# Other places in the order for loads, maxima, bulk transfers and the norm's chunks in a windowed attention stage

## The chip, the core and the metric

The kernel runs on one core of a Trainium2 chip. Its engines work side by side, each through its own list of instructions in order: TensorE (PE; weight loads are shown as PEld), VectorE (DVE), ScalarE (ACT), GpSimd (POOL) and SyncE (SP). In this kernel every DMA is issued by SP, one after the other. The metric is the time of one execution in microseconds (us) on the device; lower is better. An order of instructions is fixed when the program is built, so what the change moves are places in these five lists.

## The reference, cut to what matters

The input is 2048 rows of 448 numbers. A condition vector gives six modulation vectors. The block normalises the rows, scales and shifts them, applies attention with 16 heads of 28 numbers in which a row sees itself and the 255 rows before it, projects, adds; then it normalises again and applies a dense layer, Mish, a second dense layer, and adds.

```python
idx = jnp.arange(S)                                    # S = 2048, W = 256
mask = (idx[:, None] - idx[None, :] >= 0) & (idx[:, None] - idx[None, :] < W)
scores = jnp.where(mask[None, None], jnp.einsum("bhqd,bhkd->bhqk", q, k) * (Dh ** -0.5), -1e9)
o = jnp.einsum("bhqk,bhkd->bhqd", _softmax(scores), v)  # H = 16, Dh = 28
x = x + ga * (o_as_rows @ wo)
h = _layernorm(x) * (1 + cb) + sb
x = x + gb * (mish(h @ w1 + b1) @ w2)
```

## The kernel before

**Stages.** The rows are worked in four groups `g` of 512. Ahead of the attention loop the weights for queries, keys and values are loaded and the first group's projections are begun. The attention loop then runs over 64 *slots* (group and head: slot i is group i // 16, head i % 16). After it the dense layers run.

**Numbers in two parts.** Products of numbers with 32 bits are made of parts, a high and a low one. Queries and keys are stored to DRAM (`scr`) in three such parts (`qk_out`, L314, whose `put` issues the stores) and read back by slot with `L(i)` (L562): one DMA for q (84 rows), one for k, into 8 buffers each.

**One slot.** `A(i, t)` (L571), t from 0 to 3, multiplies a tile of 128 queries with its 384 keys, and VectorE reduces the product to the maximum of each row. When two slots are through, `M2(pr)` (L584) turns the pair's maxima with TensorE, VectorE writes them in a high and a low part (tile `mr`), and two DMAs put these as rows 84 and 85 into the q buffers of that pair, so that the next product subtracts the maximum by itself. `B(u)` (L601) makes that product, masked, with q and k the other way round, and ScalarE takes the exponential. `PV(w)` (L627) multiplies with the values; `EV`, `E` and `E2` bring the result back and divide.

**The loop.** Four slots are a round q of 12 steps (u = 12 q + r). Step r runs `B` of slot 4q + r % 4, one of its three blocks. So the pair of maxima for slots 4q + 4 and 4q + 5 has its first reader at step 12, and the pair for 4q + 6 and 4q + 7 at step 14. The 16 calls of `A` for the next four slots are spread over steps 1 to 10: those of the first slot at steps 1 and 2, of the second at 3 to 5, of the third at 6 and 7, of the fourth at 8 to 10. `M2` of the first pair stands at step 8, of the second at step 11. Slots 4q + 8 to 4q + 11 are loaded at steps 8, 9, 10 and 11, by `load_slot`, which first makes sure with `need` that their projections are stored. The first eight slots and the first two pairs are handled ahead of the loop.

**Filling work.** Between these, `fill_main(g)` yields chunks of the next group's work (`gen_hT`: transposes of the normalised rows, four chunks; `gen_qkv`: projections; `gen_oT` and `gen_wo`: output projection of the last group), and each chunk names its cost. Each step adds `RATE[g]` (twice that in the first `FRONT[g]` steps of a group) to a credit, and chunks are emitted while it is above zero. `chunk["v"]` is how many products a chunk of `tile_mms` holds; steps 0 and 18 of a group set it. Whatever is left at the end of a group is emitted at once by `drain`. A second list, `fill_early` and `fill_late`, is moved on by one entry a step (`side_step`): loads of x (`x_load`), the norm's statistics (`gen_ln1`), modulation vectors, later the first pieces of `w1`.

**Bulk transfers.** Stores of projections, loads of x rows and weights are not issued where they arise but put on the list `later`; at steps 1 to 8 and 11 of a round one entry is taken from it. `flush` issues all of it. On SP, an instruction that waits for its data holds up all that stand behind it.

Of the kernel before, what the change touches and what calls it, by code (L numbers as in the profile page):

```python
# [51 lines left out]
def adaln_block(ctx: ExitStack, tc: tile.TileContext, x, wqkv, wo, w1, b1, w2, c, w_mod, out):  # L52
# [32 lines left out]
    def bank(tag, bufs, name):  # L85
        return PS[0].tile([128, 512], F32, name=name, tag=tag, bufs=bufs)
# [4 lines left out]
    def x_load(g):  # L91
        xin[g] = qk.tile([128, 4, 512], F32, name=f"xin{g}", tag="xin")
        for t in (0, 2):
            r = g * GT + t * 128
            dma(xin[g][:, t:t + 2, 0:D], xf[r:r + 256, :].rearrange("(t p) d -> p t d", p=128))
# [134 lines left out]
    def tr_chunk(xs, ci, p):  # L230
        for t in range(4):
            PE.transpose(p[:, t * 128:(t + 1) * 128], xs[t][:, ci * 128:(ci + 1) * 128], ident)


    def hT_hi(p, ci, hh, si):
        ACT.activation(hh[:, ci], p, AF.Identity, scale=cols[:, si + 1, ci:ci + 1], bias=cols[:, si, ci:ci + 1])

    def hT_y(p, ci, y, si):
        ACT.activation(y, p, AF.Identity, scale=cols[:, si + 1, ci:ci + 1], bias=cols[:, si, ci:ci + 1])
# [5 lines left out]
    def new_T(key, pl):  # L245
        return (pl.tile([128, 4, GT], F32R, name=f"hh{key}", tag="hh"),
                pl.tile([128, 4, GT], F32R, name=f"hl{key}", tag="hl"))
# [5 lines left out]
    def gen_ln1(g, act=False):  # L253
        def xn_tiles():
            return [xin[g][:, t] for t in range(4)]
        for r in gen_ln([xin[g][:, t, 0:D] for t in range(4)], qk, xn_tiles, f"a{g}", act):
            if r:
                XS[g] = r
            yield "dve"
# [8 lines left out]
    def gen_hT(g):  # L268
        drain(ln1[g])
        hh, hl = HT[g] = new_T(g, mid)  # L270
        for ci in range(4):
            p = bank("mm", 2, f"tr{g}{ci}")
            tr_chunk(XS[g], ci, p)
            y = qk.tile([128, 512], F32, name=f"y{g}{ci}", tag="y", bufs=2)

            def ev(p=p, ci=ci, y=y):
                hT_y(p, ci, y, 0)
                hT_hi(p, ci, hh, 0)

            def lo(ci=ci, y=y):  # L280
                POOL.tensor_tensor(hl[:, ci], y, hh[:, ci].bitcast(F32), op=ALU.subtract)
            pipe.add(2, ev, lo)
            yield 2
        ht_done.add(g)

    def finish():
# [3 lines left out]
    def drain(*gs):  # L290
        for g in gs:
            for _ in g:
                pipe.step()
# [14 lines left out]
    later = []  # L308

    def flush():  # L310
        while later:
            later.pop(0)()
# [176 lines left out]
    def gen_mod_ln2(i):  # L489
        acc = yield from gen_wm_sum(i, qk)  # L490
        yield "bank"
        p = bank("mm", 2, f"mc{i}")
        mod_cols(acc, p)
        mod_cols_out(p, i - 1)
        yield
# [62 lines left out]
    NS = NG * H  # L558
# [3 lines left out]
    def L(i):  # L562
        g, h = divmod(i, H)
        q, k = Q3[i % NQ], K3[i % NK]
        f0, f1 = h * DH, D + h * DH
        q0, k0 = g * GT, max(g * GT - W, 0)
        l0 = k0 - (g * GT - W)
        dma(q[0:84, :].bitcast(F32), scr[f0:f0 + DH, :, q0:q0 + GT].rearrange("d a n -> (d a) n"))
        dma(k[0:84, l0:].bitcast(F32), scr[f1:f1 + DH, :, k0:q0 + GT].rearrange("d a n -> (d a) n"))

    def A(i, t):  # L571
        g, h = divmod(i, H)
        q, k = Q3[i % NQ], K3[i % NK]
        if i % 2 == 0 and t == 0:
            mx[i // 2] = att.tile([128, 2, 4], F32, name=f"mx{i}", tag="mx", bufs=2)
        c0 = max(256 - 128 * t, 0) if g == 0 else 0
        p = bank("sA", 2, f"sA{i}_{t}")
        PE.matmul(p[:, c0:384], q[0:84, t * 128:(t + 1) * 128], k[0:84, t * 128 + c0:t * 128 + 384],  # L578
                  start=True, stop=True)
        DVE.tensor_tensor_reduce(out=junk[:, c0:384], in0=p[:, c0:384], in1=mask[:, c0:384], scale=1.0,  # L580
                                 scalar=-3.0e38, op0=ALU.add, op1=ALU.max,
                                 accum_out=mx[i // 2][:, i % 2, t:t + 1])
# [44 lines left out]
    def PV(w):  # L627
        q, b = divmod(w, 3)
        g, h = divmod(4 * q, H)
        if b == 0:  # L630
            pvb[q] = bank("pv", 1, f"pv{q}")
        for n, (jj, t0, t1, c) in enumerate(by_width(units(g, b))):
            j = 4 * g - 2 + jj
            for a in range(4):
                PE.matmul(pvb[q][32 * a:32 * a + 32, t0 * 128:t1 * 128], V[j % NV][:, h + a, :],  # L635
                          Pt[4 * w + a][:, c:c + 128 * (t1 - t0)],
                          start=(b == 0 and n == 0), stop=False, skip_group_check=True)

    def EV(q):
        O4[q] = att.tile([128, GT], F32, name=f"o4_{q}", tag="o4")  # L640
        ACT.activation(O4[q], pvb[q], AF.Copy)
# [207 lines left out]
    def fill_early():  # L849
        yield from ln1[1]  # L850
        for g, mods in ((2, (gen_mod_wo,)), (3, (lambda: gen_mod_ln2(3), lambda: gen_mod_ln2(4)))):
            while g - 1 not in ht_done:
                yield
            for _ in range(0):
                yield
            later.append(lambda: x_load(g))
            for _ in range(6):
                yield
            flush()
            yield from ln1[g]  # L860
            for m in mods:
                yield from m()
# [8 lines left out]
    def side_step(g, two):  # L871
        i = g == NG - 1
        if not (told.get(i) == "bank" and pipe.held() or told.get(i) == "dve" and two):
            told[i] = next(side[i], None)

    RATE = (0.68, 0.93, 0.93, 0.45)
    FRONT = (0, 2, 2, 0)
    ln1 = {g: gen_ln1(g) for g in range(1, NG)}
    fillers = {g: fill_main(g) for g in range(NG)}
    side = (fill_early(), fill_late())  # L880

    def step(g):
        return next(fillers[g], 99.0) or RATE[g]

    def need(keys, g):
        if all((g, m) in done for m in keys):
            return
        flush()
        while not all((g, m) in done for m in keys):
            pipe.step()  # L890
            try:
                next(fillers[max(g - 1, 0)])
            except StopIteration:
                next(fillers[g])
            flush()

    def load_slot(i):
        if i >= NS:
            return
        g, h = divmod(i, H)  # L900
        f0, f1 = h * DH, D + h * DH
        need({f0 // 128, (f0 + 27) // 128, f1 // 128, (f1 + 27) // 128}, g)
        L(i)
# [21 lines left out]
    for u in range(NU + 7):  # L925
        s, k = divmod(u, 3)
        g = s // H
        if k == 0 and s % H == 0 and 0 < g < NG:
            drain(fillers[g - 1], *side[:g == NG - 1])
            flush()  # L930
        pipe.step()
        w, m = divmod(u - 5, 4)
        if m == 0 and 0 <= w < NU // 4:
            PV(w)
            if w % 3 == 2:
                EV(w // 3)
        if u < NU:
            B(u)
        q, r = divmod(u, 12)
        tiles = [divmod(n, 4) for n in range(16) if 1 + n * 10 // 16 == r and 4 * q + 4 < NS]  # L940
        for a, t in tiles[:1]:
            A(4 * q + 4 + a, t)
        if r in (8, 11) and 4 * q + 4 < NS:
            M2(2 * q + 2 + (r == 11))
        a = (r - 8) % 12
        if a < 4:
            load_slot(4 * ((u - 8) // 12) + 8 + a)
        if r - 3 in (0, 1) and 0 <= (u - 12 - 3) // 12 < NS // 4:
            (E, E2)[r - 3](q - 1)
        if g < NG:  # L950
            v = u - 48 * g
            if v in (0, 18):
                chunk["v"] = 4 if v == 0 and g or 0 < g < NG - 1 else 2
            if v == 0:
                credit = 0.0
            credit += RATE[g] * (2 if v < FRONT[g] else 1)
            while credit > 0.0:
                credit -= step(g)
            if v > 1:
                side_step(g, len(tiles) > 1)  # L960
            if later and r in (1, 2, 3, 4, 5, 6, 7, 8, 11):
                later.pop(0)()
        if u == NU:
            drain(fillers[NG - 1], side[1])
            while pipe.items:
                pipe.step()
            flush()
        if u - NU in TAIL:
            TAIL[u - NU]()
        for a, t in tiles[1:]:  # L970
            A(4 * q + 4 + a, t)
# [98 lines left out]
```

## Time and profile before

| | |
|---|---|
| median of 3 runs | 722.69 us (721.83 to 724.25) |
| the profiled execution | 724.64 us |
| its span, first to last instruction | 722.8 us |
| TensorE busy | 663.8 us, 92% of the span |
| VectorE, ScalarE, GpSimd busy | 349.0, 281.9, 98.2 us |
| mean granted TensorE clock | 0.970 |
| DMA | 83.79 MB, mean 116 GB/s |

The profile has a page and views that can be asked of the same trace. In a row of the waits stand the waiting instruction, what released it, the sum in us, how often, and the longest. In the timeline stand start, length, engine, line, operation and tiles, and in brackets the idle time ahead of it with the releaser. In the chain of waits in order of time stand start, length and what it was; a piece named DMA runs from the issue of the transfer to the release of what waited for it. In the table of stretches stand the stretch, its length, then for PE, PEld, DVE, ACT and POOL the busy time and the number of instructions, the granted clock, the DMA share and GB/s. A name such as `q<-mr` is a transfer or an operation that writes tile q from tile mr. Ends of matmuls are modelled, so short gaps of TensorE are known to some tenths of a microsecond only.

### The profile page before, as it was taken

How to read it: one execution, taken by the hardware profiler on the slowest of the kernel's cores; microseconds unless marked ns; L12 is line 12 of the kernel's file. 1: busy time of each engine (PE TensorE's matmuls, PEld its weight loads, DVE VectorE, ACT ScalarE, POOL GpSimd, SP SyncE). 2: the span in 40 equal slices, each digit the busy share in tenths (PEclk: the TensorE clock that was granted, in tenths of full speed). 3: DMA queues.
4: the chain of work that ended last, by engine and by line, in shares of the span. 5: the costliest groups of instructions: out<-in, count | busy, mean ns of one | idle time of the engine just before them, and what ended most of it. 6: DMA issues, size and time to landing. Idle time of an engine off the chain costs nothing.

```text
span 722.8 us, 10902 instructions
## 1 busy us (share of the span) xinstructions
PE 663.8 (92%) x3905; PEld 529.2 (73%) x3905; DVE 349.0 (48%) x934; ACT 281.9 (39%) x480; POOL 98.2 (14%) x150
## 2 busy tenths in 40 slices
PE   3876999879999899998988899999999999999996
PEld 3764566666777777776765588888888888888885
DVE  4845476644668566566656832434223222322112
ACT  3514344364444544353433673343223222422221
POOL 4632010043000200000000125422010000000002
PEclk9998899989999899999998999999999999999999
DMA  7666466456745546644275166300300020001001
GB/s 203 195 197 211 139 177 221 126 139 185 230 164 156 158 124 198 223 135 150 75 213 150 58 211 172 105 12 0 103 0 1 4 100 0 1 10 42 1 0 52
DMA packets 48114, 83.79 MB, mean 116 GB/s; under 512 B 6126, under 2 KB 26108, under 8 KB 48060
## 3 DMA queue, kind: packets, MB, share of 16 engines
q1 hardware_dynamic: 48060, 83.10, 37.5%
q8 instruction: 31, 0.51, 0.3%
q14 instruction: 23, 0.19, 0.1%
HBM read 53.45 MB, written 29.36 MB: 115 GB/s over the span
## 4 chain that ended last, share of the span: by engine, by line
PE 67%; DMA 13%; issue 11%; DVE 6%; SPq 3%; ACT 0%; POOL 0%; POOLq 0%; DVEq 0%; ACTq 0%
PE z L807 15%; DMA q<-mr 9%; PE qk L300 6%; PE sA L578 6%; PE sB L622 6%; PE acc L990 5%; PE acc L991 5%; PE acc L989 5%; PE pv L635 4%; PE wo L300 4%; PE sB L620 3%; PE qk_v L300 3%; SPq L59 3%; DVE junk L580 1%; DMA wm<-in_w_mod_dram 1%
## 5 line engine op out<-in xcount | busy, mean ns | idle before, releaser
L580 DVE CUSTOM_DVE_ANT_0 junk<-sA,mask 128x384 bf16<-128x384 f32 (+2 forms) x256 | 135.7, 530 | 131.9 <-PE sA L578 119.6
L625 ACT ACTIVATE P<-sB 128x512 f32<-128x512 f32 (+2 forms) x192 | 109.0, 572 | 171.0 <-PE sB L622 166.2
L815 DVE TENSOR_TENSOR al<-t,ah 128x512 fp32r<-128x512 f32 x56 | 38.8, 693 | 202.0 <-ACT ah L814 202.0
L622 PE MATMUL sB<-q,k 86*128 86x384 f32 (+1 forms) x352 | 94.3, 344 | 29.9 <-DMA q<-mr 29.9
L813 ACT ACTIVATE t<-z,b1c 128x512 f32<-128x512 f32 x56 | 38.6, 689 | 188.8 <-PE z L807 177.8
L578 PE MATMUL sA<-k,q 84*128 84x384 f32 (+2 forms) x256 | 95.3, 380 | 6.3 <-DMA k<-scr 4.5
L807 PE MATMUL z<-hhf,w 128*128 128x512 f32 x224 | 89.8, 401 | 0.0
L807 PE MATMUL z<-hlf,w 128*128 128x512 f32 x224 | 88.7, 396 | 0.0
L622 PEld LDWEIGHTS sB<-q,k 86*128 86x128 f32 x352 | 58.6, 204 | 32.7 <-DMA q<-mr 31.9
L989 PE MATMUL acc<-w2h,ah 128*128 128x448 f32 x224 | 82.1, 366 | 0.0
L990 PE MATMUL acc<-w2l,ah 128*128 128x448 f32 x224 | 82.0, 366 | 0.0
L991 PE MATMUL acc<-w2h,al 128*128 128x448 f32 x224 | 82.0, 366 | 0.0
L807 PE MATMUL z<-hhf,w1l 128*128 128x512 f32 x168 | 66.3, 395 | 0.0
L620 PE MATMUL sB<-fdmask,identr 128*128 128x128 bf16 (+1 forms) x320 | 61.7, 259 | 0.7 <-ACT P L625 0.7
L620 PEld LDWEIGHTS <-identr 128*128 128x128 bf16 x320 | 22.5, 100 | 53.7 <-issue 51.5
L578 PEld LDWEIGHTS sA<-k,q 84*128 84x128 f32 x256 | 52.0, 206 | 12.7 <-POOL k L435 4.9
L635 PE MATMUL pv<-P,v 128*32 128x256 f32 (+2 forms) x704 | 49.5, 395 | 0.0
L807 PEld LDWEIGHTS z<-hlf,w 128*128 128x128 f32 x224 | 42.2, 189 | 9.9
L807 PEld LDWEIGHTS z<-hhf,w 128*128 128x128 f32 x224 | 42.3, 189 | 8.7 <-issue 0.6
L989 PEld LDWEIGHTS acc<-w2h,ah 128*128 128x128 f32 x224 | 42.1, 188 | 5.1
L990 PEld LDWEIGHTS acc<-w2l,ah 128*128 128x128 f32 x224 | 42.1, 188 | 5.1
L991 PEld LDWEIGHTS acc<-w2h,al 128*128 128x128 f32 x224 | 42.1, 188 | 3.5
(143 smaller groups left out, 999.6 us busy)
## 6 DMA issues: line engine op xcount, KB each, us to landing
scr<-st SPq DMA_DIRECT2D x24, 512.0 KB
k<-scr SPq DMA_DIRECT2D x48, 252.0 KB
q<-scr SPq DMA_DIRECT2D x64, 168.0 KB
scr<-st SPq DMA_DIRECT2D x32, 256.0 KB
x<-x1d SPq DMA_DIRECT2D x10, 448.0 KB
xin<-in_A_x_dram SPq DMA_DIRECT2D x8, 448.0 KB
xr<-in_A_x_dram SPq DMA_DIRECT2D x16, 224.0 KB
x1d<-xr SPq DMA_DIRECT2D x16, 224.0 KB
```

The source lines that it names most:

```text
L300: PE.matmul(p, b, a, start=(n == 0), stop=(n == 10))
L578: PE.matmul(p[:, c0:384], q[0:84, t * 128:(t + 1) * 128], k[0:84, t * 128 + c0:t * 128 + 384], start=True, stop=True)
L580: DVE.tensor_tensor_reduce(out=junk[:, c0:384], in0=p[:, c0:384], in1=mask[:, c0:384], scale=1.0, scalar=-3.0e38, op0=ALU.add, op1=ALU.max ...
L620: PE.matmul(p[:, c:c + n], identr, fdmask[:, m:m + n], start=(i == 0), stop=False, skip_group_check=True)
L622: PE.matmul(p[:, c:c + 128 * (t1 - t0)], k[:, jj * 128:(jj + 1) * 128], q[:, t0 * 128:t1 * 128], start=False, stop=True, skip_group_check= ...
L625: ACT.activation(P[:, c0:], p[:, c0:], AF.Exp, scale=SCALE)
L635: PE.matmul(pvb[q][32 * a:32 * a + 32, t0 * 128:t1 * 128], V[j % NV][:, h + a, :], Pt[4 * w + a][:, c:c + 128 * (t1 - t0)], start=(b == 0 ...
L807: PE.matmul(zb[n], ps[m][1], ps[m][0], start=(m == 0), stop=(m == 10))
L815: DVE.tensor_tensor(al[n], t, ah[n].bitcast(F32), op=ALU.subtract)
L989: PE.matmul(p, ah[n][:, ts], w2h[f], start=(f == 0), stop=False)
L990: PE.matmul(p, ah[n][:, ts], w2l[f], start=False, stop=False)
L991: PE.matmul(p, al[n][:, ts], w2h[f], start=False, stop=(f == NF - 1))
```

## The change

It touches the attention loop's order alone; what is computed stays the same.

```diff
@@ gen_hT
-            yield 2
+            yield 2.5
@@ fill_early
-            for _ in range(0):
+            for _ in range(2):
                 yield
             later.append(lambda: x_load(g))
@@ rates
-    RATE = (0.68, 0.93, 0.93, 0.45)
-    FRONT = (0, 2, 2, 0)
+    RATE = (0.68, 1.01, 0.93, 0.45)
+    FRONT = (0, 1, 3, 0)
@@ the loop
-        if r in (8, 11) and 4 * q + 4 < NS:
+        if r in (7, 11) and 4 * q + 4 < NS:
             M2(2 * q + 2 + (r == 11))
-        a = (r - 8) % 12
-        if a < 4:
-            load_slot(4 * ((u - 8) // 12) + 8 + a)
+        for a in range(4):
+            if (u - (8, 11, 14, 16)[a]) % 12 == 0 and u >= (8, 11, 14, 16)[a]:
+                load_slot(4 * ((u - (8, 11, 14, 16)[a]) // 12) + 8 + a)
...
-            if v in (0, 18):
+            if v in (0, 2):
                 chunk["v"] = 4 if v == 0 and g or 0 < g < NG - 1 else 2
...
-            if later and r in (1, 2, 3, 4, 5, 6, 7, 8, 11):
+            if later and r in (1, 4, 5, 6, 8, 9):
                 later.pop(0)()
```

- **Loads.** The four slots of a round, loaded at steps 8, 9, 10, 11, are loaded at 8, 11, 14 and 16, that is, the last two at steps 2 and 4 of the next round. At step 11 the load stands behind `M2`, as before.
- **Maxima.** `M2` of the first pair goes from step 8 to step 7; the second stays at step 11.
- **Bulk transfers.** The list `later` is served at steps 1, 4, 5, 6, 8 and 9.
- **The norm's chunks.** A chunk of `gen_hT` counts 2.5 instead of 2; a load of x rows goes on the list two entries of the side list later.
- **Filling work.** In group 1 the rate is 1.01 instead of 0.93 and one first step instead of two counts double; in group 2 three first steps do. The size of the chunks of products is set at steps 0 and 2 instead of 0 and 18 of a group; this makes a difference in group 3 alone, where it falls from 4 to 2 products at step 2.

## The prediction

> **What bounds the kernel now.** I read the page's chain of work by line first, then the waits of TensorE, then the SP queue around one wait, then the chain again in order of time.
>
> ```profile
> PE z L807 15%; DMA q<-mr 9%; PE qk L300 6%; PE sA L578 6%; PE sB L622 6%; PE acc L990 5%; PE acc L991 5%; PE acc L989 5%; PE pv L635 4%; PE wo L300 4%; PE sB L620 3%; PE qk_v L300 3%; SPq L59 3%; DVE junk L580 1%; DMA wm<-in_w_mod_dram 1%
> ```
>
> The chain that ended last is TensorE's own work, and the one transfer of weight in it is `q<-mr`, the row of maxima, 4 KB each. Next come TensorE's waits over the whole span, and the stretch of the attention loop.
>
> ```profile
> PE sB L622 <- DMA q<-mr: 29.9, 14, 4.7
> ```
>
> ```profile
> 48.00:418.00 370.00, 335.20 (x2369) 246.64 (x2368) 233.03 (x745) 165.40 (x294) 35.80 (x47) 0.95 0.52 160
> ```
>
> In 370.0 us TensorE (first pair of numbers) is busy for 335.2. Of the 34.8 us left, 29.9 are 14 waits of a `B` product for maxima. VectorE is busy for 233.0 and ScalarE for 165.4, so neither is next in line: whatever TensorE doesn't wait for, it gains.
>
> Why are 4 KB late? The SP queue in one round of 12 steps (start, length, transfer):
>
> ```profile
> 213.30 0.41 SPq L59 DMA_DIRECT2D q<-scr  x1
> 213.76 0.38 SPq L59 DMA_DIRECT2D k<-scr  x1
> 214.23 0.34 SPq L59 DMA_DIRECT2D q<-scr  x1
> 214.62 0.38 SPq L59 DMA_DIRECT2D k<-scr  x1
> 215.65 0.31 SPq L59 DMA_DIRECT2D q<-scr  x1
> 216.01 0.38 SPq L59 DMA_DIRECT2D k<-scr  x1
> 217.33 1.38 SPq L59 DMA_DIRECT2D q<-mr  x2
> 218.80 0.41 SPq L59 DMA_DIRECT2D q<-scr  x1
> 219.26 0.38 SPq L59 DMA_DIRECT2D k<-scr  x1
> ```
>
> ```profile
> scr<-st SPq DMA_DIRECT2D x24, 512.0 KB
> k<-scr SPq DMA_DIRECT2D x48, 252.0 KB
> q<-scr SPq DMA_DIRECT2D x64, 168.0 KB
> scr<-st SPq DMA_DIRECT2D x32, 256.0 KB
> ```
>
> Three slots' loads (steps 8, 9, 10; by the page's part on DMA issues, above, 168 + 252 = 420 KB a slot) stand right ahead of the second pair of maxima (step 11), whose reader is the `B` of step 14. The chain of waits gives the time from the issue of the pair's second row to the release of that `B` (start, length); these are its ten longest pieces between 60 and 420 us:
>
> ```profile
> 86.00 4.39 DMA q<-mr
> 106.33 4.16 DMA q<-mr
> 125.85 4.97 DMA q<-mr
> 146.30 5.39 DMA q<-mr
> 170.30 5.06 DMA q<-mr
> 241.20 5.06 DMA q<-mr
> 290.68 4.32 DMA q<-mr
> 337.49 6.29 DMA q<-mr
> 361.66 5.48 DMA q<-mr
> 385.64 4.24 DMA q<-mr
> ```
>
> and in the last round, which loads no slots any more, with the first k load of the program beside it:
>
> ```profile
> 39.76 4.72 DMA k<-scr
> ```
>
> ```profile
> 406.82 1.76 DMA q<-mr
> ```
>
> Alone the row takes 1.76 us; behind three loads 4.16 to 6.29. So 2.4 to 4.5 us of each are queueing. Starts of neighbouring rows give the round: 146.30 - 125.85 = 20.5 us, 170.30 - 146.30 = 24.0 us; a step is 1.7 to 2.0 us.
>
> **The change part by part.**
>
> *Loads.* Of each round's four slots, the first keeps step 8, the second goes from 9 to 11 (behind the second pair of maxima), the third and fourth from 10 and 11 to steps 2 and 4 of the next round. Ahead of the second pair there is now one slot's load, issued three steps (5.1 to 6.0 us) before, instead of three slots' loads. 1.26 MB cost up to 6.29 - 1.76 = 4.5 us, so one slot costs up to 1.5 and is through by then. I take the queueing as gone.
>
> How much of the wait goes with it? In the round shown, the second row is issued at 217.33 + 0.74 = 218.07 (the two halves of 1.38 and the step between); with 1.76 it would be there at 219.83.
>
> ```profile
> 221.68 0.41 PE L622 MATMUL sB<-q,k 86*128 86x384 f32 x1 [0.88 <-DMA q<-mr]
> ```
>
> TensorE came to it at 221.68 - 0.88 = 220.80, so the row would be 1.0 us early and the whole 0.88 goes. Over the middle of the loop (80 to 380 us) and for the worst place behind it:
>
> ```profile
> PE sB L622 <- DMA q<-mr: 21.6, 11, 3.7
> ```
>
> ```profile
> 390.02 0.66 PE L622 MATMUL sB<-q,k 86*128 86x384 f32 x1 [3.17 <-DMA q<-mr]
> ```
>
> The longest wait of the eleven, 3.7, meets queueing of 5.39 - 1.76 = 3.6 or 6.29 - 1.76 = 4.5, and the others are shorter; I count the 21.6 as gone but for 0.1. At 390.02 queueing was 4.24 - 1.76 = 2.5 of 3.17 us: 2.5 goes, 0.7 stays. The first wait of the loop, the 4.7 us of the waits' row, stays: its pair follows slots 4 to 7, which the code ahead of the loop loads and the diff leaves alone. The remaining wait, 29.9 - 21.6 - 3.2 - 4.7 = 0.4, is the one of the last round without loads and stays. **Saved: 21.5 + 2.5 = 24.0 us.**
>
> *Clock.* After the longer waits the granted clock (the number behind the busy times) is 0.50. This is one such stretch, and the sum of all five that follow waits which I count as gone:
>
> ```profile
> 246.00:252.80 6.80, 6.41 (x26) 5.69 (x26) 3.67 (x11) 3.21 (x6) 2.04 (x2) 0.50 0.31 100
> ...
> sum 27.20, PE 24.76 PEld 21.77 DVE 12.43 ACT 10.26 POOL 3.76; mean PE 4.95 PEld 4.35 DVE 2.49 ACT 2.05 POOL 0.75
> ```
>
> The wait ahead of the one shown, and one after which the clock held, with the stretch behind it:
>
> ```profile
> 246.39 0.66 PE L622 MATMUL sB<-q,k 86*128 86x384 f32 x1 [2.34 <-DMA q<-mr]
> ```
>
> ```profile
> 130.96 0.41 PE L622 MATMUL sB<-q,k 86*128 86x384 f32 x1 [1.87 <-DMA q<-mr]
> ```
>
> ```profile
> 132.00:136.00 4.00, 4.00 (x30) 2.60 (x29) 3.59 (x13) 1.27 (x3) 0.00 (x0) 1.00 0.40 150
> ```
>
> A wait of 1.87 us left the clock at 1.00, one of 2.34 did not. What stays in those five places is under 1 us, so the half-speed stretches go. TensorE was busy for 24.76 us in them, at full clock half of that: **12.4 us saved.** Bounds: 0 if other idle time trips the clock anyway, 24.76 / 2 if not; I take the upper end, since 1.87 held.
>
> The Trainium skill ("TensorE: Matmul & The Clock Gate", section "HAM oscillation — how this bites in real kernels") says that it takes idle gaps of over about 3.4 us to halve the clock. By that, the stretch behind the 2.34 us wait isn't due to the wait and its 6.41 / 2 = 3.2 us stay; this trace's 2.34 speaks against it, so the sum keeps them.
>
> *The second slot's load.* It now follows the maxima at step 11 and its first product is at step 3 of the next round, four steps on instead of six. Nothing in the loop waits for a load today, so the price has to be bounded. The fourth slot's load stood in just this place, issued 218.80 to 219.26; the second slot's first product was here:
>
> ```profile
> 223.25 0.39 PE L578 MATMUL sA<-k,q 84*128 84x384 f32 x1
> ```
>
> Without the 0.88 us wait it starts at 222.37, 3.1 us after the k issue. A landing takes between 1.76 (the small row) and 4.72 us (the k load above, itself behind others): a wait between none and 1.6 us, on TensorE, with all products behind it. Rounds with longer steps (24.0 against 20.5 us) have more room. I take the middle, 0.7 us, in six of the rounds: **4 us given back** (both ends: 0 and 15 x 1.6 = 24). The third and fourth slots keep four steps from issue to use, with no bulk transfer between the two loads; 4 x 1.7 = 6.8 us cover 4.72, cost nothing, and 2 us a round if stores at step 1 hold them.
>
> *Maxima.* The first pair goes from step 8 to 7. None of the fourteen waits is its own in the middle of the loop (each row above is a second pair's), so nothing is gained there; its VectorE reductions end at step 5, which hides the move. It also lets SP reach the first slot's load sooner. 0 us; 0.9 us a round (a wait like that of 0.88) if VectorE is late.
>
> *Bulk transfers.* They may leave at six steps of twelve (1, 4, 5, 6, 8, 9) instead of nine; step 9 is new, 11 is gone. A store of 768 KB (512 and 256, the first and last of the four issue rows above) costs 0.77 / 1.26 x 4.5 = 2.7 us of the queue, with the first slot's load 4.2, less than the 5.1 to 6.0 us from step 8 to 11. Cost 0; if two stores leave there, 6.9, up to 1.8 us of wait in that round.
>
> *Norm and fillers.* x loads start two steps later and may wait for an allowed step: at worst 2 steps (3.9 us) are left for 0.9 MB (0.9 / 1.26 x 4.5 + 1.8 = 5.0 us), 1.1 us of VectorE twice. The chunks' cost 2 to 2.5, the rate 0.93 to 1.01, the doubled first steps, and the smaller groups of the last stage move the same products among steps; TensorE does them all, so their time is hidden by nothing and changed by nothing but idle time. I put all of this at +1 us (between -3 and +6).
>
> **Sum.** The profiled execution took 724.64 us (span 722.8). 724.6 - 24.0 - 12.4 + 4 + 1 = 693.2. It is 1.95 us above the median of the runs, 722.69, so on their footing **691.2 us**.
>
> **Rivals.**
>
> 1. *Half is given back.* The second slot waits 1.6 us in most rounds and two stores sometimes meet the second pair: 12 x 1.6 = 19 instead of 4, so 706 us. For it: 4.72 for a k load, and no spare time in the round shown. Against it: no load has been late in the loop so far, and with three loads gone from ahead the queue is shorter.
>
> 2. *Slower.* The second slot's load, issued behind the maxima at step 11, is late wherever stores left at steps 8 and 9. About eight of the rounds have a store there (two of six allowed places; 4 x 7 tiles less the three ahead of the loop are 25 stores); at 2 x 2.7 us of queue less the time that passes, each costs 3 us of wait and then a half-speed stretch of 3.4 us, so 1.7 more: 8 x 4.7 = 38 us, and with the 5 of the other terms kept and 36 saved the time is 730 us. It decides from (36.4 - 5) / 8 = 3.9 us a round on. Against it: 5.1 to 6.0 us lie between. The Trainium skill ("DMA: Bandwidth & Descriptors", section "Rules for kernel authors") advises to issue a transfer early and wait late, and three of four loads go the other way. Here, a third slot was issued at 215.65 and first used at 229.70, so early issue bought 14 us that nobody needed.
>
> ```profile
> 229.70 0.34 PE L578 MATMUL sA<-k,q 84*128 84x384 f32 x1
> ```
>
> 3. *It doesn't do it.* The pair is late by its own way (transpose, two VectorE operations, two issues) and not by the queue: 722.7 us. Against it: 1.76 alone, and 1.0 us to spare in the round shown.
>
> 4. *More.* The head of the loop gains too, its 4.7 us wait and half of the slow stretch behind it, and no load waits: 724.6 - 24.0 - 12.4 - 4.7 - 5 - 1.95 = 677 us.
>
> **How the numbers follow.** Forecast (684 to 699 us) 0.58; half given back (699 to 715) 0.22; more (below 684) 0.08; no effect 0.04; slower 0.08. The range leaves out the far half of the cases on either side: 682 to 710 us. A measurement of this kernel can tell about 0.3% from no change; the three chances are faster 0.58 + 0.22 + 0.08 = 0.88, within 0.04, slower 0.08.
>
> **What would show it.** Right: TensorE's waits for `q<-mr` fall from 29.9 to about 6 us, the longest still that at the head of the loop; the chain's `q<-mr` pieces are near 1.8 us; clock 1.00 from 90 us on; a new row `PE sA L578 <- DMA k<-scr` or `q<-scr` of some 4 us. Wrong: that row over 15 us; `q<-mr` over 15 us with one load ahead of it; VectorE waiting for `xin`; 0.50 stretches without a long wait ahead.

## The result, and the profile after

The changed kernel takes 700.62 us (median of 4 runs, 700.13 to 703.91) against 723.47 us before (721.83 to 725.19): 22.9 us less between the medians. The ratio of the runs is 0.969, with a 95% interval of 0.965 to 0.973, so 3.1% less. The forecast was 691.2 us, in a range from 682 to 710. The profiled execution of the changed kernel has a span of 698.3 us, 24.5 less than the 722.8 of before.

The chain of work by line, after:

```profile
PE z L807 16%; PE qk L300 9%; PE sA L578 6%; PE pv L635 6%; PE sB L622 5%; PE wo L300 5%; PE acc L990 5%; PE acc L991 5%; PE acc L989 5%; PE sB L620 4%; PE qk_v L300 4%; DMA k<-scr 2%; SPq L59 2%; DVE junk L580 2%; DMA wm<-in_w_mod_dram 1%
```

`q<-mr`, 9% of the span before, is no longer among the lines shown; `k<-scr` is new with 2%. TensorE's waits after (sum, times, longest):

```profile
PE sA L578 <- DMA k<-scr: 9.8, 4, 4.8
PE sB L622 <- DMA q<-mr: 5.1, 3, 4.1
PE sA L578 <- DVE mx L580: 3.9, 11, 0.8
```

The waits for maxima fell from 29.9 to 5.1 us, and 4.1 of those are the one at the head of the loop. The longest wait for k, and the longest in the loop, are these:

```profile
44.44 0.77 PE L578 MATMUL sA<-k,q 84*128 84x128 f32 x2 [4.82 <-DMA k<-scr]
```

```profile
145.77 0.41 PE L578 MATMUL sA<-k,q 84*128 84x384 f32 x1 [3.10 <-DMA k<-scr]
```

The first stands ahead of the loop, as it did before, so 9.8 - 4.8 = 5.0 us are new. They are three waits, of 3.10, 1.10 and 0.81 us. The piece of the chain behind the longest shows the issue of the second slot's k and the time until its reader was released:

```profile
140.25 5.38 DMA k<-scr
```

That load stands behind the second pair, which left only at 138.34 us, and the third and fourth slots' loads were issued right behind it (140.73 to 142.37), although their steps come later: SP had been held at the pair for 3.6 us, until VectorE had written it. The row of waits for `mx` read so before:

```profile
PE sA L578 <- DVE mx L580: 1.5, 6, 0.4
```

One round of the SP queue after, at the place of the one shown of before:

```profile
201.50 1.38 SPq L59 DMA_DIRECT2D q<-mr  x2
202.97 0.41 SPq L59 DMA_DIRECT2D q<-scr  x1
203.44 0.89 SPq L59 DMA_DIRECT2D k<-scr  x1
208.96 1.38 SPq L59 DMA_DIRECT2D q<-mr  x2
210.43 0.41 SPq L59 DMA_DIRECT2D q<-scr  x1
210.89 0.38 SPq L59 DMA_DIRECT2D k<-scr  x1
```

One slot's load stands ahead of the second pair, issued 6.0 us before it (202.97 to 208.96); before, three stood there and the first was issued 4.0 us ahead (213.30 to 217.33). The loop as a whole, from its first exponential to its last, before and after (stretch, length, TensorE's busy time first):

```profile
63.50:418.10 354.60, 321.69 (x2301) 236.27 (x2300) 220.71 (x701) 160.29 (x288) 32.29 (x40) 0.95 0.52 160
```

```profile
64.60:393.00 328.40, 312.15 (x2301) 226.64 (x2300) 218.48 (x701) 159.39 (x288) 32.11 (x40) 0.98 0.57 173
```

The loop is 26.2 us shorter. TensorE's idle time in it fell from 32.9 to 16.3 us, and it runs the same 2301 products in 9.5 us less. The clock accounts for them. Before, six stretches of the loop had half the clock, 34.45 us of busy time by the five summed in the prediction and this first one:

```profile
68.50:78.70 10.20, 9.69 (x38) 6.82 (x39) 3.73 (x16) 3.61 (x8) 1.27 (x1) 0.50 0.55 183
```

After, there are three:

```profile
67.70:74.50 6.80, 5.01 (x23) 3.34 (x23) 2.43 (x10) 2.70 (x5) 0.37 (x2) 0.50 0.51 178
146.20:149.60 3.40, 3.40 (x25) 2.85 (x27) 1.39 (x6) 1.76 (x3) 0.00 (x0) 0.50 0.62 163
374.90:378.30 3.40, 3.40 (x24) 1.81 (x24) 1.69 (x7) 0.98 (x2) 0.24 (x1) 0.50 0.26 66
sum 13.60, PE 11.81 PEld 8.00 DVE 5.51 ACT 5.44 POOL 0.60; mean PE 3.94 PEld 2.67 DVE 1.84 ACT 1.81 POOL 0.20
```

If half the clock doubles the time of a product, half of the difference, (34.45 - 11.81) / 2 = 11.3 us, is what the clock gave; 16.6 us of idle time and these make 27.9, of which 26.2 are seen. Where the other 1.7 went isn't shown; products that overlap a little worse are one guess.

### The profile page after: what moved, and what is told of

Same layout as the page of the kernel before. It is cut to its first block, busy times and chain, and to the rows that moved or that the text cites. A ratio compares the mean times of both kernels' runs of the same rounds, so it can differ in the third digit from the quotient of the medians.

```text
span 698.3 us, 10903 instructions
## 1 busy us (share of the span) xinstructions
PE 655.8 (94%) x3905; PEld 520.5 (75%) x3905; DVE 346.6 (50%) x934; ACT 280.8 (40%) x480; POOL 98.2 (14%) x150
## 4 chain that ended last, share of the span: by engine, by line
PE 74%; issue 11%; DMA 6%; DVE 5%; SPq 2%; ACT 0%; POOL 0%; POOLq 0%; DVEq 0%; ACTq 0%
PE z L807 16%; PE qk L300 9%; PE sA L578 6%; PE pv L635 6%; PE sB L622 5%; PE wo L300 5%; PE acc L990 5%; PE acc L991 5%; PE acc L989 5%; PE sB L620 4%; PE qk_v L300 4%; DMA k<-scr 2%; SPq L59 2%; DVE junk L580 2%; DMA wm<-in_w_mod_dram 1%
## 5 line engine op out<-in xcount | busy, mean ns | idle before, releaser
L578 PE MATMUL sA<-k,q 84*128 84x384 f32 (+2 forms) x256 | 91.6, 368 | 14.8 <-DMA k<-scr 9.8
L622 PE MATMUL sB<-q,k 86*128 86x384 f32 (+1 forms) x352 | 90.7, 332 | 5.1 <-DMA q<-mr 5.1
L578 PEld LDWEIGHTS sA<-k,q 84*128 84x128 f32 x256 | 49.2, 195 | 24.2 <-DVE mx L580 11.7
L620 PE MATMUL sB<-fdmask,identr 128*128 128x128 bf16 (+1 forms) x320 | 60.3, 254 | 0.7 <-ACT P L625 0.7
L622 PEld LDWEIGHTS sB<-q,k 86*128 86x128 f32 x352 | 55.9, 195 | 6.2 <-DMA q<-mr 5.1
```

Of the source, the lines that this page charges most:

```text
L620: PE.matmul(p[:, c:c + n], identr, fdmask[:, m:m + n], start=(i == 0), stop=False, skip_group_check=True)
L622: PE.matmul(p[:, c:c + 128 * (t1 - t0)], k[:, jj * 128:(jj + 1) * 128], q[:, t0 * 128:t1 * 128], start=False, stop=True, skip_group_check= ...
```

## The experiments

The theory: the second pair of maxima is late because loads stand ahead of it in one queue, and the change gains by taking them away. The rivals: another of the three other parts carries the gain (first pair earlier, bulk transfers, fillers with the norm's chunks), or only the set does. So each part was tried alone and, in the changed kernel, undone alone; then the places that still wait were tried. Each ratio is to the kernel before on the same chip, whose median was between 722.4 and 726.3 us, so kernels compare by their ratios rather than by their times. The waits are TensorE's in us; those for `k<-scr` are counted from 50 us on, because the one ahead of the loop (2.8 to 4.8 us) stands in every kernel and is put down to another releaser in some.

| kernel | us | ratio (95% interval) | wait `q<-mr` | wait `k<-scr` in the loop |
|---|---|---|---|---|
| changed | 700.6 | 0.969 (0.965 to 0.973) | 5.1 | 5.0 |
| loads alone | 709.4 | 0.982 (0.978 to 0.986) | 5.9 | 9.3 |
| all but loads | 716.0 | 0.991 (0.988 to 0.994) | 20.1 | none |
| bulk alone | 741.2 | 1.025 (1.020 to 1.030) | 38.2 | none |
| fillers alone | 736.5 | 1.019 (1.014 to 1.025) | 32.1 | 0.3 |
| first pair alone | 710.2 | 0.983 (0.976 to 0.989) | 16.7 | 0.5 |
| changed, first pair back | 706.0 | 0.977 (0.971 to 0.984) | 5.8 | 7.0 |
| changed, bulk back | 710.3 | 0.983 (0.978 to 0.989) | 5.1 | 13.0 |
| changed, fillers back | 708.2 | 0.978 (0.971 to 0.985) | 5.9 | 9.7 |
| changed, second slot at 9 | 695.9 | 0.958 (0.953 to 0.964) | 6.9 | 0.7 |
| changed, head of the loop | 698.1 | 0.962 (0.958 to 0.966) | 2.4 | 4.0 |
| changed, products later | 706.9 | 0.974 (0.970 to 0.978) | 4.9 | 1.7 |
| both of the last two | 702.8 | 0.969 (0.965 to 0.974) | 2.9 | 1.5 |

**The loads alone.**

```diff
 # the kernel before
-        a = (r - 8) % 12
-        if a < 4:
-            load_slot(4 * ((u - 8) // 12) + 8 + a)
+        for a in range(4):
+            if (u - (8, 11, 14, 16)[a]) % 12 == 0 and u >= (8, 11, 14, 16)[a]:
+                load_slot(4 * ((u - (8, 11, 14, 16)[a]) // 12) + 8 + a)
```

> The kernel before with the loads' new steps alone (8, 11, 14, 16). Queue theory: nearly the whole gain comes from here; TensorE's waits for q<-mr fall from 29.9 to about 6 us, waits for k<-scr of some 5 us appear, time 699 to 706 us. Rival (the gain needs the other places too, above all the bulk transfers away from steps 2, 3 and 11): over 711 us.

709.4 us. Its waits of TensorE:

```profile
PE sA L578 <- DMA k<-scr: 12.1, 9, 2.8
PE sB L622 <- DMA q<-mr: 5.9, 3, 4.9
```

The waits for maxima are gone as the theory has it, but the time falls between theory and rival: 13 us of 22.9. Waits for k came in their place, eight in the loop (9.3 us) and the one ahead of it. The loads free the pair by themselves; they don't make the gain by themselves.

**All but the loads.**

```diff
 # the changed kernel
-        for a in range(4):
-            if (u - (8, 11, 14, 16)[a]) % 12 == 0 and u >= (8, 11, 14, 16)[a]:
-                load_slot(4 * ((u - (8, 11, 14, 16)[a]) // 12) + 8 + a)
+        a = (r - 8) % 12
+        if a < 4:
+            load_slot(4 * ((u - 8) // 12) + 8 + a)
```

> The changed kernel with the loads back at steps 8, 9, 10, 11. Queue theory: the maxima stand behind three loads again, waits for q<-mr 24 to 30 us, time 718 to 724 us. Rival: maxima at step 7, bulk transfers and fillers carry a good part by themselves, under 712 us.

716.0 us and 20.1 us of waits for maxima: neither theory. Something else than the loads takes a third of these waits away; the run with the first pair alone, below, finds it.

**The bulk transfers alone.**

```diff
 # the kernel before
-            if later and r in (1, 2, 3, 4, 5, 6, 7, 8, 11):
+            if later and r in (1, 4, 5, 6, 8, 9):
```

> The kernel before with the bulk transfers' new steps alone. Queue theory: within 3 us of before (720 to 726 us), since three loads still stand ahead of the second pair. Rival: stores at steps 2, 3 and 11 were part of the queue, under 718 us.

741.2 us, 2.5% slower: both theories miss it. The SP queue ahead of a second pair, and the chain's piece for it:

```profile
123.72 0.42 SPq L59 DMA_DIRECT2D q<-scr  x1
124.19 0.37 SPq L59 DMA_DIRECT2D k<-scr  x1
124.65 0.89 SPq L59 DMA_DIRECT2D scr<-st  x2
125.64 1.13 SPq L59 DMA_DIRECT2D q<-scr  x1
126.82 1.05 SPq L59 DMA_DIRECT2D k<-scr  x1
127.92 0.40 SPq L59 DMA_DIRECT2D wm<-in_w_mod_dram  x1
128.42 0.41 SPq L59 DMA_DIRECT2D q<-scr  x1
128.87 0.39 SPq L59 DMA_DIRECT2D k<-scr  x1
129.36 1.37 SPq L59 DMA_DIRECT2D q<-mr  x2
```

```profile
130.09 6.21 DMA q<-mr
```

A store and a piece of weights (`wm`) now leave between the loads. The pair of this round stood behind three loads and a piece of weights before, 4.97 us; with the store added it takes 6.21. Between the two pairs of a round stand the bulk transfers of steps 8 and 9. Step 8 was there before and step 9 is new; over 14 rounds 18 bulk transfers stand there instead of 6. They are bad places while the three loads are there too. The waits for maxima grew by 8.3 us, and the granted clock of the profiled execution fell from 0.970 to 0.950; the rest of the loss is not taken apart.

**The fillers alone** (with the norm's chunks and the x load).

```diff
 # the kernel before
-            yield 2
+            yield 2.5
...
-            for _ in range(0):
+            for _ in range(2):
...
-    RATE = (0.68, 0.93, 0.93, 0.45)
-    FRONT = (0, 2, 2, 0)
+    RATE = (0.68, 1.01, 0.93, 0.45)
+    FRONT = (0, 1, 3, 0)
...
-            if v in (0, 18):
+            if v in (0, 2):
```

> The kernel before with the norm's chunks, the later x load, the rates, the first steps and the chunk sizes of the change alone. Queue theory: within 4 us of before (719 to 727 us), waits for q<-mr 25 us or more. Rival: more filling work ahead of the waiting product covers the wait, under 717 us.

736.5 us, 1.9% slower, with 32.1 us of waits for maxima, 2.2 more than before. The theory was right on the wait and wrong on the time. The loss goes with the clock: the mean granted clock was 0.949 to 0.959 in its four runs and 0.963 to 0.972 in the seven of the kernel before beside them. The profiled execution, the fastest of the four, has 7.6 us more span, and TensorE's busy time at half the clock is longer by 3.6 us in the loop (38.1 against 34.5) and by 9.5 us ahead of it. Half of these 13.1 us and the 2.2 us of waits cover the 7.6. Why the clock fell isn't settled.

**The first pair alone.** Two parts alone lose and the set without loads gains, so the part left over had to gain.

```diff
 # the kernel before
-        if r in (8, 11) and 4 * q + 4 < NS:
+        if r in (7, 11) and 4 * q + 4 < NS:
```

> The kernel before with the first pair of maxima at step 7 alone. The earlier runs left this part alone to explain why all parts but the loads gain 6 us while bulk places alone and fillers alone lose. Theory: at step 8 SP holds the first slot's load until the first pair's rows are issued (two issues and the wait for VectorE); from step 7 the loads start some 2 us earlier and the queue has drained further when the second pair comes. Waits for q<-mr fall from 29.9 to 18 to 24 us, 711 to 718 us. Rival (nothing waits for the first pair, so its place is free): 720 to 725 us.

710.2 us. The waits for maxima, and a round of the SP queue:

```profile
PE sB L622 <- DMA q<-mr: 16.7, 10, 4.1
```

```profile
207.23 1.36 SPq L59 DMA_DIRECT2D q<-mr  x2
208.69 0.41 SPq L59 DMA_DIRECT2D q<-scr  x1
...
212.98 0.38 SPq L59 DMA_DIRECT2D k<-scr  x1
214.30 1.36 SPq L59 DMA_DIRECT2D q<-mr  x2
```

Six loads still stand between the pairs, but the first is issued 5.6 us ahead of the second pair (208.69 to 214.30) instead of 4.0. Over 14 rounds the first load is issued 4.7 us ahead in the mean instead of 3.4. No product waits for the first pair. It is SP that waits: it holds at a pair until VectorE has written it, and the loads behind it are held too. This is SP's row for both pairs of a round, before:

```profile
SPq L59 <- DVE mr L589: 120.7, 26, 14.0
```

One step earlier gives the queue 1.6 us more to drain in the round shown, and 13 of the 29.9 us of waits go. The theory holds.

**Undoing one part of the changed kernel.** The first pair back at step 8:

```diff
-        if r in (7, 11) and 4 * q + 4 < NS:
+        if r in (8, 11) and 4 * q + 4 < NS:
```

> The changed kernel with the first pair back at step 8. Theory: only one slot's load lies ahead of the second pair here, so the first pair's place matters little: waits for q<-mr under 8 us, 700 to 705 us. Rival (its place carries several us in any order): over 707 us.

706.0 us, waits for maxima 5.8. With one load in the queue the earlier start is hardly needed for the second pair. The ratio is higher by some 5 us, but its interval overlaps that of the changed kernel, so this is not shown. The bulk transfers back:

```diff
-            if later and r in (1, 4, 5, 6, 8, 9):
+            if later and r in (1, 2, 3, 4, 5, 6, 7, 8, 11):
```

> The changed kernel with the bulk transfers back at steps 1 to 8 and 11. Theory: stores leaving at steps 11, 2 and 3 now stand between the loads, as in the run with the loads alone, where TensorE's waits for k<-scr came to 12.1 us against 9.8: waits for k<-scr over 12 us, 704 to 710 us. Rival (bulk places matter only with three loads ahead of the maxima): within 2 us of the changed kernel, 699 to 703 us.

710.3 us, some 10 us of the gain gone, and TensorE's waits for k are 17.0, of which 13.0 lie in the loop, against 5.0 in the changed kernel:

```profile
PE sA L578 <- DMA k<-scr: 17.0, 9, 3.9
```

The same steps for the bulk transfers that cost 18 us alone are worth 10 in the set. With loads at steps 11, 2 and 4, stores at 11, 2 and 3 can stand between them, and a load is now needed four steps after its issue; the longer waits for k fit this, but single waits weren't traced to a store. The fillers back:

```diff
-            yield 2.5
+            yield 2
...
-            for _ in range(2):
+            for _ in range(0):
...
-    RATE = (0.68, 1.01, 0.93, 0.45)
-    FRONT = (0, 1, 3, 0)
+    RATE = (0.68, 0.93, 0.93, 0.45)
+    FRONT = (0, 2, 2, 0)
...
-            if v in (0, 2):
+            if v in (0, 18):
```

> The changed kernel with chunks, x load, rates, first steps and chunk sizes back as before. Theory: fillers only decide how much room a load or a pair has, not what stands in the queue: 699 to 706 us, waits for q<-mr under 8 us. Rival (as part of the set they carry several us): over 708 us.

708.2 us, with runs from 701.7 to 710.0, and 9.7 us of waits for k in the loop. Its interval, 0.971 to 0.985, meets that of the changed kernel, so whether fillers carry anything in the set stays open; that they lose 14 us alone does not carry over.

**The second slot back at step 9.** This undoes one of the four loads' moves.

```diff
 # the changed kernel, at all three places
-(8, 11, 14, 16)[a]
+(8, 9, 14, 16)[a]
```

> The changed kernel with the second slot's load back at step 9, ahead of the second pair of maxima. Theory (a trade between the two waits): two slots' loads lie ahead of the pair, so its wait grows, waits for q<-mr 7 to 14 us, while waits for k<-scr fall to the 5 us ahead of the loop; time 700 to 706 us. Rival (the wait for k at step 3 was the larger loss): under 698 us.

695.9 us; the rival is right.

```profile
PE sB L622 <- DMA q<-mr: 6.9, 5, 3.8
PE sA L578 <- DMA k<-scr: 5.2, 3, 4.5
```

Leaving out the longest of each row, which stand at the head of the loop and ahead of it, the loop now waits 3.1 us for maxima (1.0 in the changed kernel) and 0.7 for k (5.0). Two loads drain in time as well, with the first pair at step 7; it was the third and fourth that had to go. The interval, 0.953 to 0.964, lies just below that of the changed kernel, 0.965 to 0.973. It is the lowest ratio of all that ran, though it can't be told from the next kernel's (0.958 to 0.966).

**The head of the loop.**

```diff
 # the changed kernel
-        load_slot(4 + i)
+        if i < 2:
+            load_slot(4 + i)
...
-        for a in range(4):
-            if (u - (8, 11, 14, 16)[a]) % 12 == 0 and u >= (8, 11, 14, 16)[a]:
-                load_slot(4 * ((u - (8, 11, 14, 16)[a]) // 12) + 8 + a)
+        for a, d in enumerate((8, 11, 2, 4)):
+            if r == d and (a > 1 or u >= d):
+                load_slot(4 * (u // 12) + (8 if a < 2 else 6 - 2) + a)
```

> The changed kernel with slots 6 and 7 loaded at steps 2 and 4 of the first round instead of ahead of the loop. Theory: the 4.1 us wait at the head of the loop is the same queue (two slots' loads and stores ahead of the pair): it falls by about 1.5 us or more, with part of the half-speed stretch behind it; 695 to 699 us. Rival (the stores alone hold the pair): 699 to 702 us.

698.1 us; the wait at the head falls from 4.1 to 1.4.

```profile
PE sB L622 <- DMA q<-mr: 2.4, 3, 1.4
```

The same queue, so the same cure. But the half-speed stretch behind the wait, which was to shrink, is longer than in the changed kernel, with TensorE busy at half the clock for 13.20 us instead of 5.01:

```profile
65.80:79.40 13.60, 13.20 (x54) 8.49 (x54) 5.62 (x24) 4.75 (x10) 2.54 (x2) 0.50 0.43 131
```

So in the profiled execution the stretch costs 4.1 us more than there and the shorter wait saves 2.7. And the ratio's interval, 0.958 to 0.966, just meets the changed kernel's: a gain of some 5 us is likely, not shown.

**The products of the second slot later.**

```diff
 # the changed kernel
-        tiles = [divmod(n, 4) for n in range(16) if 1 + n * 10 // 16 == r and 4 * q + 4 < NS]
+        tiles = [divmod(n, 4) for n in range(16) if 2 + n * 9 // 16 == r and 4 * q + 4 < NS]
```

> The changed kernel with the products A of the second slot at steps 4 and 5 instead of 3 to 5 (all sixteen spread over steps 2 to 10). Theory: the load at step 11 then has five steps, 1.5 to 2 us more than it lacked, so waits for k<-scr in the loop (5.0 us) go to under 1 us with the half-speed stretch behind the longest, 694 to 698 us. Rival (VectorE has less time for the reductions before the pair is turned): waits for mx rise over 6 us and the time stays at 699 us or more.

706.9 us, where 694 to 698 were expected, though the wait it aimed at went. The ratio, 0.974, is above the changed kernel's 0.969, with intervals that overlap: no gain, and a loss that isn't shown.

```profile
PE sA L578 <- DMA k<-scr: 6.2, 4, 4.5
PE sB L622 <- DMA q<-mr: 4.9, 2, 4.1
PE sA L578 <- DVE mx L580: 3.3, 11, 0.9
PE tr L232 <- DVE xin L222: 2.8, 1, 2.8
```

1.7 us for k in the loop instead of 5.0, and no more on `mx` than the 3.9 of the changed kernel, so the rival's mechanism is not it. A wait for normalised rows (2.8) is new, with 6.4 us of TensorE's busy time at half the clock behind it, and so is the length of this stretch at half the clock, with no wait over 1 us ahead of it:

```profile
378.70:389.00 10.30, 9.98 (x57) 5.53 (x56) 6.90 (x23) 3.01 (x6) 1.14 (x4) 0.50 0.01 3
```

It costs 5 us, against 1.7 for the stretch at this place in the changed kernel (374.90). The stretch at the head of the loop has 12.0 us of busy time instead of 5.0. In all TensorE is busy at half the clock for 28.4 us of the loop instead of 11.8, which is some 8 us, and the two profiled executions are 7.8 us apart: the clock took more than the wait for k gave. The other runs agree, with mean granted clocks of 0.969 to 0.981 in the six and 0.979 to 0.983 in the four of the changed kernel. The wait for normalised rows comes with the order, since the next kernel has it too (2.8); whether the other two stretches do, the runs don't show.

**Both.** The last two edits together.

> Both of the last two edits. If they act in different places, as the theory says, their gains add: 691 to 696 us.

702.8 us (701.7 to 705.6), 4 less than with the later products alone (704.3 to 709.8), so the head's gain adds to those. The range of 691 to 696 us is missed all the same, as the range of the later products alone was.

## Why the prediction was right, and where it was not

- **The forecast as a whole: right way and inside the range, but short.** 22.9 us of the 31.5 forecast came. 700.6 us lies beyond the 684 to 699 of the main forecast, in the band of the rival "half is given back" (699 to 715). That rival's mechanism, 12 waits of 1.6 us for the second slot, did not come: there were three, of 5.0 us in all.
- **The queue ahead of the second pair: right in mechanism and size.** 24.0 us of waits were to go, 24.8 went; the wait at the head stayed, as said. The loads alone do it (5.9 left).
- **The clock: near in size (12.4 forecast, 11.3 found) with some luck, wrong in its rule.** The five stretches went, as forecast. But the one at the head, which was left out of the sum, gave (9.69 - 5.01) / 2 = 2.3 us, and the two at 146.2 and 374.9 us took (3.40 + 3.40) / 2 = 3.4. So the sign "clock 1.00 from 90 us on" failed, and the stretch at 374.9 is what the prediction listed as a sign of being wrong: 0.50 without a long wait ahead. "A wait of 1.87 us left the clock at 1.00, one of 2.34 did not" is no threshold. In the run with the first pair alone a wait of 1.59 us was followed by half the clock:

```profile
241.92 0.47 PE L622 MATMUL sB<-q,k 86*128 86x384 f32 x2 [1.59 <-DMA q<-mr]
```

```profile
243.70:247.10 3.40, 3.40 (x21) 2.88 (x24) 2.42 (x9) 2.37 (x5) 1.46 (x1) 0.50 0.01 3
```

- **The second slot's load: 4 us forecast, 5.0 found.** That the sums agree is partly luck: six waits of 0.7 us were priced, with 1.6 as the upper end, and three came, the longest 3.10 with a landing of 5.38 us, above the 4.72 taken as the worst. Behind that wait the clock then halved (146.20), another 1.7 us. What the price left out is SP's hold at the second pair, behind which three slots' loads left almost together; with the second slot ahead of the pair the waits for k in the loop are 0.7 us. The price was taken from one place; it hangs on what leaves beside the loads (13.0 us in the loop with the old bulk steps), and the move needn't have been made at all.
- **The first pair, "0 us": wrong.** I looked for who waits for the pair and found nobody; the sentence that it "lets SP reach the first slot's load sooner" had the mechanism and no price. Alone it is worth 13 us. It can't have spoiled the sum much: with the loads gone the waits for maxima are 5.8 us without it and 5.1 with it.
- **Bulk transfers, "Cost 0": wrong both ways.** Some 18 us lost alone, 10 gained in the set.
- **Fillers, between -3 and +6: wrong for the part alone (+14), open in the set.**
- **The size.** The terms came to 31.4 us less than the profiled execution; its successor has 24.5 less. Of the 6.9 missing, other idle time in the loop is 16.3 - 5.1 - 5.0 = 6.2 instead of 32.9 - 29.9 = 3.0, so 3.2 more, mostly waits for `mx` (3.9 against 1.5) which came up when the longer ones went; 1.8 are the part of TensorE's busy time that stays unexplained; 1.7 lie outside the loop (26.2 there, 24.5 in all), most of it ahead of the loop, where the granted clock from 40 us on was 0.86 instead of 0.93; 1.1 are missing at the clock and 1.0 at the loads; against these stand 0.8 more of saved waits and the 1 us counted for the rest, which leaves 7.0. "Whatever TensorE doesn't wait for, it gains" was the sentence that was too simple: VectorE is busy for 62 to 67% of the loop, and that is enough to be next in single places.

## What to carry to other kernels

In a queue that is served in order, price a moved instruction by what stands behind it, not by who waits for it: the first pair had no waiter and was worth 13 us, because SP stood still at it. Places in such an order don't add up: four parts that gain 13, 13, -18 and -14 us alone make about 23 together, so measure a part inside the set as well as alone, and don't discard a step because it loses by itself. And when a small urgent transfer is late, first take away the last loads ahead of it; here, with the first pair earlier, the third and fourth slots were enough, and moving the second as well cost more than it gave.

## What the runs showed of the hardware

- The half-speed stretch at the head of the loop doesn't follow the length of the wait there. Behind waits of 4.1, 4.7 and 4.1 us TensorE is busy at half the clock for 5.01 (changed), 9.69 (before) and 14.07 us (bulk back, the row below), and behind the 1.4 us of the run with the head of the loop for 13.20:

```profile
64.90:82.00 17.10, 14.07 (x58) 9.21 (x59) 5.63 (x24) 4.71 (x10) 2.48 (x2) 0.50 0.34 120
```

  Between 5.01 and 14.07 us of busy time at half the clock lie 4.5 us of span, and the runs don't show what sets them. So a few microseconds between two single profiles are no proof of what an edit does.
- The half-speed stretches in the rows above last 3.40, 6.80, 10.20, 10.30, 13.60 and 17.10 us, near multiples of 3.4. In the longest without large gaps, 378.70 to 389.00 with the products later, TensorE is busy for 9.98 of 10.30 us and the clock still stays at 0.50.
- After the long waits went, the clock still fell to half once, at 374.9 us, with no wait over 1 us ahead of it for 10 us. Many short gaps seem to do it as one long one does; the runs don't separate the two.
